# First factor of a Fourier transform: rows n1 and 47-n1 in separate 32x32 tiles, joined on VectorE

## The chip, the cores and the metric

The kernel runs on one core of one Trainium2 chip. The metric is device time in microseconds (us); all arithmetic is FP32. TensorE (PE in the profile) multiplies into PSUM banks, ScalarE (ACT) and VectorE (DVE) move and combine what stands there, GpSimd (POOL) and SyncE (SP) issue DMAs.

## The reference

Eight sequences of 3008 rows and 256 columns are filtered in the frequency domain, and the result goes through a two-layer network with an ELU in between.

```python
batch, seq, dim = (8, 3008, 256)          # x: batch x seq x dim
X = np.fft.rfft(x, axis=1)
F = (filt_r + 1j * filt_i)[None, :, :]    # seq // 2 + 1 frequencies
y = np.fft.irfft(X * F, n=x.shape[1], axis=1).astype(np.float32)
x = y.reshape(8 * 3008, 256)
h = x @ w_in                              # 256 -> 2048
g = np.where(h > 0.0, h, np.exp(np.minimum(h, 0.0)) - 1.0)
out = (g @ w_out).astype(np.float32)      # 2048 -> 256
```

## The kernel before

3008 is 47 x 64. The forward transform of a batch is made in two factors. The first (`a_unit`, line 236) multiplies the 64 rows n2 of one residue n1 by a table of 64 columns; rows n1 and 47-n1 use the same angles with opposite sign, so they are loaded together. The 24 pairs of residues are 6 chunks of 4 (`c` from 0 to 5). `x_load` (lines 205 to 216) brings a chunk into tile `xc` and its table into `ta`. `x_unit` (lines 222 and 223) forms on DVE the sum `sd` and the difference of the two halves of the 64 rows, which gives even and odd frequencies. Of a chunk's four pairs (slots), two lie on the lower and two on the upper 64 partitions; of each 64, 32 hold rows n1 and 32 rows 47-n1. `a_unit` takes two chunks and contracts those 64 together: the table has the columns cosine and sine twice, once with the sign that joins the two residues. The products land as 64x64 tiles, four at a time, in two banks per chunk, and ACT copies the four banks into two tiles `t1` (line 240). `z_write` (line 310) writes each chunk with two DMAs into the scratch `z` in DRAM, and `z_read` (line 316) reads it back transposed into the tile `t2`.

The second factor, `b_unit` (line 385), runs in sixteen 32x32 tiles at once, one bank for each row of tiles, ACT copies (line 390) and DVE sums (lines 403 and 404). `re_mult`, `re_sums`, `im_mult`, `im_join`, `im_sums` apply the filter on DVE, `bi_unit` (line 457) transforms back by the first inverse factor, again in sixteen tiles, `y_write` (line 468) and `y_read` (lines 487 and 491) pass through DRAM, and `n_unit` (line 524) makes the last inverse factor, six blocks `m` per batch, with sums on DVE (`n_sums`, lines 547 and 549).

The network works on blocks of 512 tokens by a seven-product scheme (Strassen's) in both layers. An item is one block `m` and one quarter `q` of the hidden layer, 24 items per batch. `up_steps` gives seven products into the banks called `s`, `a` and `d` (line 572), with copies on ACT (line 583), ELU exponentials on ACT (lines 589 and 590), sums (line 580) and maxima (line 594) on DVE and a tail of DVE differences (lines 630 to 634); `down_steps` gives seven products of the item before into four accumulators `po` (line 654), which are copied and joined (lines 659 and 670), transposed on DVE (line 693) and written out (line 703).

Four PSUM banks, handed out in a fixed order by the list `banks`, serve the up products and all transform stages; the other four are `po`.

The order is written out by hand. One loop step, called a quad in the code, interleaves the seven up products (U) of an item with the seven down products (D) of the item before. `at(quad, place, fn, ...)` plans other work into it: place 0 is the middle of the quad, place 1 its end, 2 and 3 points in between. A quad named in `opens` starts with D, because a stage at the end of the quad before has taken all four banks. The transform of batch `b` runs in the 24 quads in which the network works on batch `b - 1`; batch 0 has a transform of its own ahead of the loop (`a_first`, `b_first`, `bi_first`), beside which the weights are decoded (`w_split`, `w_float`, `w_join`, `w_sums`), some of that into the first quads of batch 1. Within a batch's 24 quads `a_unit` stands at the end of three quads, with `z_write`, `z_read` and the next `x_load`s behind it:

```python
for c, s in enumerate((2, 2, 3, 3, 4, 4) if b == 1 else (0, 0, 3, 3, 4, 4)):
    at(t + s, 0, x_unit, b, c)
    if c % 2 == 0:
        opens.add(t + s + 1)
        at(t + s, 1, a_unit, b, c)
```

`b_unit` stands at the end of quads 6, 10, 14 and 18, `bi_unit` at the end of quads 9, 13, 17 and 21, `n_unit` in the middle of quads 23, 1, 5, 8, 12 and 16. In all there are 21 `a_unit`s: three in each of batches 1 to 7.

## Time and profile before

| | |
|---|---|
| time, median of 3 runs | 2563.08 us (2561.91 to 2564.88) |
| the profiled execution: its span, first to last instruction | 2560.5 us |
| granted TensorE clock, mean of the span | 0.996 |
| PE, DVE, ACT busy | 98%, 81%, 60% of the span |
| L236 (`a_unit`), PE | 672 records of 0.38 us, up to four at once |
| L240, ACT copies of `a_unit` | 84 of 0.60 us |
| L222, L223, DVE, `x_unit` | 84 of 0.69 us |
| L403, L404, DVE sums of `b_unit` | 112 of 0.68 to 0.69 us |
| `z` written (SP) | 84 DMAs of 256 KB |
| `z` read into `t2` (SP) | 224 DMAs of 96 KB |

The profiled execution lies 2.6 us below the median of the runs, as its span leaves out what surrounds the instructions. The trace keeps records for each instruction, so an FP32 matmul appears as two records and two weight loads. The times in a timeline count from the first instruction of the span; the loop's first quad starts at about 87 us, quad 0 of batch 2 at about 397 us.

### The profile page before, as it was taken

What the parts mean: (1) busy time and instruction counts of PE and PEld (TensorE: products, weight loads), DVE (VectorE), ACT (ScalarE), POOL (GpSimd) and SP (SyncE); (2) the same over time, 40 slices, a digit from 0 to 9 for tenths busy, and PEclk for the clock granted to TensorE, in tenths of its full rate; (3) what the DMA queues carried; (4) which work ended last, traced back from release to release, by engine and by line L of the source; (5) the groups of instructions that cost most, each with busy time, mean ns of one, the idle gap of its engine ahead of it and who ended that gap; (6) DMA issues with size and microseconds to landing.
All of it is one profiled execution on the core that took longest, in us unless ns stands there. A gap on an engine that the chain in (4) does not pass through costs nothing.

```text
span 2560.5 us, 43982 instructions
## 1 busy us (share of the span) xinstructions
PE 2520.5 (98%) x16682; PEld 2161.5 (84%) x16682; DVE 2067.5 (81%) x3578; ACT 1545.2 (60%) x2715; POOL 159.5 (6%) x315
## 2 busy tenths in 40 slices
PE   6999999999999999999999999999999999999998
PEld 4788889888898888988889888888889888898887
DVE  6978887788878888788877888778897788876766
ACT  7766556655566555666566656566655665555554
POOL 5001000000000000000000000000100010000000
PEclk8999999999999999999999999999999999999999
DMA  9662223523233221433225231343213322110010
GB/s 283 182 184 67 58 45 79 131 62 71 48 100 97 69 66 40 128 80 72 52 52 142 66 77 36 77 123 80 66 39 84 88 62 63 37 45 18 20 27 17
DMA packets 229879, 200.56 MB, mean 78 GB/s; under 512 B 129398, under 2 KB 201990, under 8 KB 229668
## 3 DMA queue, kind: packets, MB, share of 16 engines
q1 hardware_dynamic: 214308, 166.86, 26.6%
q0 software_dynamic: 14000, 30.44, 4.2%
q8 instruction: 131, 2.15, 0.3%
q14 instruction: 80, 0.66, 0.1%
q10 hardware_dynamic: 1360, 0.46, 0.1%
HBM read 125.80 MB, written 78.12 MB: 80 GB/s over the span
## 4 chain that ended last, share of the span: by engine, by line
PE 97%; DMA 2%; DVE 1%; issue 0%; ACT 0%; SPq 0%; DVEq 0%; ACTq 0%
PE po L654 45%; PE phs L572 25%; PE phd L572 13%; PE pha L572 6%; PE psn L524 2%; PE psa L236 2%; PE pf L385 1%; PE pv L457 1%; DMA xc<-in_x_dram 1%; PE po L332 1%; DMA x<-in_x_dram 0%; PE po L298 0%; PE psr L332 0%; DMA t<-yd 0%; PE psa L279 0%
## 5 line engine op out<-in xcount | busy, mean ns | idle before, releaser
L654 PE MATMUL po<-g,wo 128*128 128x256 f32 (+1 forms) x5376 | 1317.6, 377 | 0.0
L654 PEld LDWEIGHTS po<-g,wo 128*128 128x128 f32 x5376 | 1010.7, 190 | 165.9 <-issue 49.8
L583 ACT ACTIVATE g<-phs 128x512 f32<-128x512 f32 (+1 forms) x576 | 338.7, 588 | 735.3 <-PE phs L572 733.3
L590 ACT ACTIVATE e<-e 128x512 f32<-128x512 f32 (+1 forms) x768 | 477.2, 621 | 24.3
L594 DVE SCALAR_TENSOR_TENSOR g<-e,g 128x512 f32<-128x512 f32 (+1 forms) x576 | 387.5, 673 | 13.6 <-ACT e L590 13.2
L580 DVE TENSOR_TENSOR g<-phd,g 128x512 f32<-128x512 f32 (+1 forms) x384 | 258.9, 674 | 166.2 <-ACT e L590 108.7
L572 PE MATMUL phs<-y,wi 128*128 128x256 f32 (+1 forms) x1536 | 387.6, 375 | 0.1
L572 PE MATMUL phd<-y,wi 128*128 128x256 f32 (+1 forms) x1504 | 380.3, 375 | 0.0
L589 ACT ACTIVATE e<-g 128x512 f32<-128x512 f32 (+1 forms) x576 | 354.4, 615 | 34.2 <-DVE g L580 26.7
L572 PEld LDWEIGHTS phs<-y,wi 128*128 128x128 f32 x1536 | 291.4, 190 | 33.6 <-ACT y L507 0.3
L572 PEld LDWEIGHTS phd<-y,wi 128*128 128x128 f32 x1504 | 284.8, 190 | 35.1 <-DVE g L580 2.7
L594 DVE SCALAR_TENSOR_TENSOR g<-e,phs 128x512 f32<-128x512 f32 (+1 forms) x192 | 129.8, 676 | 115.1 <-ACT e L590 115.1
L572 PE MATMUL phs<-yt,wi 128*128 128x256 f32 (+1 forms) x768 | 193.9, 375 | 0.9 <-ACT g L583 0.9
L572 PE MATMUL phs<-yb,wi 128*128 128x256 f32 (+1 forms) x768 | 193.9, 375 | 0.6 <-ACT g L583 0.6
L572 PE MATMUL pha<-yb,wi 128*128 128x256 f32 (+1 forms) x736 | 186.0, 375 | 0.0
L589 ACT ACTIVATE e<-phs 128x512 f32<-128x512 f32 (+1 forms) x192 | 112.2, 584 | 112.0 <-PE phs L572 112.0
L580 DVE TENSOR_TENSOR g<-pha,g 128x512 f32<-128x512 f32 (+1 forms) x192 | 129.5, 674 | 44.9 <-PE pha L572 44.9
L572 PEld LDWEIGHTS phs<-yt,wi 128*128 128x128 f32 x768 | 145.7, 190 | 18.0 <-ACT g L583 1.5
L572 PEld LDWEIGHTS phs<-yb,wi 128*128 128x128 f32 x768 | 143.1, 190 | 20.2 <-ACT g L583 1.0
L326 POOL DMA_DIRECT2D fall<-fp x224 | 110.1, 499 | 723.5 <-DVE r L430 697.7
L572 PEld LDWEIGHTS pha<-yb,wi 128*128 128x128 f32 x736 | 139.3, 190 | 16.7 <-ACT fall L394 0.5
L631 DVE TENSOR_TENSOR g<-g,g 128x512 f32<-128x512 f32 (+1 forms) x192 | 130.7, 681 | 6.7
(166 smaller groups left out, 2064.9 us busy)
## 6 DMA issues: line engine op xcount, KB each, us to landing
yd<-t SPq DMA_DIRECT2D x127, 192.0 KB
t<-yd SPq DMA_DIRECT2D x92, 256.0 KB
z<-t SPq DMA_DIRECT2D x84, 256.0 KB
fall<-fp POOLq DMA_DIRECT2D x224, 96.0 KB, 2.9
t<-z SPq DMA_DIRECT2D x224, 96.0 KB
out_dram<-o SPq DMA_DIRECT2D x632, 32.0 KB
xc<-in_x_dram SPq DMA_DIRECT2D x84, 128.0 KB
xc<-in_x_dram SPq DMA_DIRECT2D x161, 64.0 KB
```

The lines of the kernel that those rows point to most:

```text
L236: nc.tensor.matmul(p[o:o + 64, u, :], w[r, u, o:o + 64], src[r, u, :], start=True, stop=True)
L326: nc.gpsimd.dma_start(t[32 * a:32 * a + 24].rearrange("p c u d -> p (c u d)"), fp[g, a].rearrange("q c u d -> q (c u d)"))
L332: nc.tensor.matmul(ps[:, u:u + w, :], table[k, v, :], r[k, u:u + w, :], start=n == 0, stop=n == len(rhs) - 1)
L524: nc.tensor.matmul(p[ts(c, 64), dh, ts(q, 64)], t[r, i - 4 * m, ds(dh * P + 64 * c, 64)], w[r, i - 4 * m, :], start=True, stop=True)
L572: nc.tensor.matmul(ps[:, a, 0:h], w_in[q][:, COMBO[n], a, :], y[n], start=start and a == 0, stop=True, skip_group_check=True)
L580: nc.vector.tensor_tensor(out=g[o], in0=i0, in1=i1, op=ALU.add)
L583: nc.scalar.activation(out=g[o], in_=i0, func=AXT.Copy)
L589: nc.scalar.activation(out=e, in_=src, func=AXT.Relu, scale=-1.0)
L590: nc.scalar.activation(out=e, in_=e, func=AXT.Exp, scale=-1.0)
L594: nc.vector.scalar_tensor_tensor(out=g[n], in0=es[n], scalar=1.0, in1=src, op0=ALU.subtract, op1=ALU.max)
L631: nc.vector.tensor_tensor(out=b12, in0=b22, in1=b12, op=ALU.subtract)
L654: nc.tensor.matmul(po[i][:, u, 0:h], w_out[q][:, COMBO[n], a, :], g[n][:, a, :], start=q == 0 and a == 0 and n in (1, 3, 6, 4), stop=True, ...
```

## The change

Rows n1 and 47-n1 are no longer contracted in 64-row tiles with the joining sign in the table. Each of the four groups of 32 partitions (`k`: rows n1 and rows 47-n1 of the lower and of the upper two slots) is a row of 32x32 tiles with a bank of its own; the four columns of tiles are two chunks (`j`) by sum and difference (`o`). So the table `ta` keeps every second block of 32 columns (64 columns instead of 128). A unit issues 32 matmuls of 256 columns instead of 16, first those of rows 0 to 2, then those of row 3, for each of two slots `u`. Afterwards ACT copies two banks instead of four (1 and 3), and DVE forms the sum and the difference of each copied bank with its neighbour (0 and 2), into the tile `t1`, which now holds two slots of both chunks. The banks go back in the order 1, 3, 0, 2.

The scratch `z` becomes `[24, 2, 65, 256]`, sum and difference apart. `z_write` handles two chunks in one call, with eight DMAs of 128 KB instead of two times two of 256 KB; `z_read` takes the same four blocks of 24 rows from their new places. In batch 1 the three stages move by one quad, from quads 2, 3 and 4 to 3, 4 and 5; the other batches keep theirs.

```diff
-    ta = np.ascontiguousarray(tb).reshape(P, H // 2, P)
+    ta = np.ascontiguousarray(tb[..., 0::2, :]).reshape(P, H // 2, 64)
...
     def a_unit(b, c):
-        ps = [[bank("psa") for _ in range(2)] for _ in range(2)]
-        for j in range(2):
-            xt, w, sm = xs.pop((b, c + j)), tas.pop((b, c + j)), sds.pop((b, c + j))
-            for u in range(2):
-                for o, src in ((0, sm), (64, xt[:, 1])):
-                    for (_, p), r in zip(ps[j], HALVES):
-                        nc.tensor.matmul(p[o:o + 64, u, :], w[r, u, o:o + 64], src[r, u, :], start=True, stop=True)
-        for j in range(2):
-            t = t1s[b, c + j] = t1p.tile([P, XC, D], FP32, tag="t1", name="t1")
-            for h, (i, p) in enumerate(ps[j]):
-                nc.scalar.activation(out=t[:, 2 * h:2 * h + 2, :], in_=p, func=AXT.Copy)
-                banks.append(i)
+        ps = [bank("psa") for _ in range(4)]
+        src = [(tas.pop((b, c + j)), (sds.pop((b, c + j)), xs.pop((b, c + j))[:, 1])) for j in range(2)]
+        for u in range(2):
+            for rows in ((0, 1, 2), (3,)):
+                for j, (w, parts) in enumerate(src):
+                    for o in range(2):
+                        for k in rows:
+                            r, a = slice(32 * k, 32 * k + 32), 64 * j + 32 * o
+                            nc.tensor.matmul(ps[k][1][a:a + 32, u, :], w[r, u, 32 * o:32 * o + 32], parts[o][r, u, :],
+                                             start=True, stop=True, tile_position=(32 * k, a))
+        for h in range(2):
+            t = t1s[b, c, h] = t1p.tile([P, XC, D], FP32, tag="t1", name="t1").rearrange("p (u s) d -> p u s d", s=2)
+            one, two = ps[2 * h][1], ps[2 * h + 1][1]
+            nc.scalar.activation(out=t[:, :, 1], in_=two, func=AXT.Copy)
+            nc.vector.tensor_tensor(out=t[:, :, 0], in0=t[:, :, 1], in1=one, op=ALU.add)
+            nc.vector.tensor_tensor(out=t[:, :, 1], in0=one, in1=t[:, :, 1], op=ALU.subtract)
+        banks.extend(ps[k][0] for k in (1, 3, 0, 2))
...
     def z_write(b, c):
         if c == 0:
-            zs[b] = zp.tile([H, 4 * K2 + 1, D], FP32, tag="z", name="z")
-        t = t1s.pop((b, c))
-        z = zs[b][XC * c:XC * c + XC, 0:4 * K2, :].rearrange("i (q r) d -> r q i d", r=2)
-        for r in range(2):
-            nc.sync.dma_start(z[r], t[HALVES[r]])
+            zs[b] = zp.tile([H, 2, 2 * K2 + 1, D], FP32, tag="z", name="z")
+        for h in range(2):
+            t = t1s.pop((b, c, h)).rearrange("p u s d -> p (u s) d")
+            for j in range(2):
+                i = XC * (c + j) + 2 * h
+                z = zs[b][i:i + 2, :, 0:2 * K2, :].rearrange("i s (q r) d -> r q (i s) d", r=2)
+                for r in range(2):
+                    a = 64 * j + 32 * r
+                    nc.sync.dma_start(z[r], t[a:a + 32])
...
-                for c, s in enumerate((2, 2, 3, 3, 4, 4) if b == 1 else (0, 0, 3, 3, 4, 4)):
+                for c, s in enumerate((3, 3, 4, 4, 5, 5) if b == 1 else (0, 0, 3, 3, 4, 4)):
...
                     if c % 2:
-                        for k in (c - 1, c):
-                            at(t + s, 1, z_write, b, k)
+                        at(t + s, 1, z_write, b, c - 1)
```

More of the change, by code (lines that the diff above doesn't have):

```diff
@@ L201, in x_load @@
     def x_load(b, c, queue=nc.sync, place=None):
-        t, w = place or (xp.tile([P, 2, 2, D], FP32, tag="xc", name="xc"), tap.tile([P, 2, P], FP32, tag="ta", name="ta"))
+        t, w = place or (xp.tile([P, 2, 2, D], FP32, tag="xc", name="xc"), tap.tile([P, 2, 64], FP32, tag="ta", name="ta"))
         xs[b, c], tas[b, c] = t, w
@@ L305, in z_write @@
         if c == 0:
-            zs[b] = zp.tile([H, 4 * K2 + 1, D], FP32, tag="z", name="z")
-        t = t1s.pop((b, c))
-        z = zs[b][XC * c:XC * c + XC, 0:4 * K2, :].rearrange("i (q r) d -> r q i d", r=2)
-        for r in range(2):
-            nc.sync.dma_start(z[r], t[HALVES[r]])
+            zs[b] = zp.tile([H, 2, 2 * K2 + 1, D], FP32, tag="z", name="z")
[7 more added lines that the diff above has]
+                    nc.sync.dma_start(z[r], t[a:a + 32])
     def z_read(b, g):
         t = t2[:, g % 2]
-        for p in range(4):
-            k = p * K2 + 4 * g
+        for p, (n, k) in enumerate(((0, 0), (1, K2), (0, K2), (1, 0))):
             nc.sync.dma_start(t[32 * p:32 * p + 24].rearrange("i u d -> i (u d)"),
-                              zs[b][:, k:k + 4, :].rearrange("i u d -> i (u d)"))
+                              zs[b][:, n, k + 4 * g:k + 4 * g + 4, :].rearrange("i u d -> i (u d)"))
     def f_read_first(g, t):
```

## The prediction

> **What bounds the kernel now.** I read the page first: span, busy shares, chain.

> ```profile
> span 2560.5 us, 43982 instructions
> ...
> PE 2520.5 (98%) x16682; PEld 2161.5 (84%) x16682; DVE 2067.5 (81%) x3578; ACT 1545.2 (60%) x2715; POOL 159.5 (6%) x315
> ...
> PE 97%; DMA 2%; DVE 1%; issue 0%; ACT 0%; SPq 0%; DVEq 0%; ACTq 0%
> ```

> TensorE ends everything: 97% of the chain. What shortens PE's own stream counts in full; DVE, at 81%, has room on average but not in every quad (one step of the item loop: 12.1 us of L572 and L654 matmuls, plus what is planned into it). Next I read PE's timeline around one `a_unit` of batch 2:

> ```profile
> 457.21 0.43 PE L236 MATMUL psa<-sd,ta 64*64 64x256 f32 x2
> ...
> 458.79 0.38 PE L236 MATMUL psa<-xc,ta 64*64 64x256 f32 x2
> 459.10 1.13 PE L654 MATMUL po<-g,wo 128*128 128x256 f32 x4
> ```

> Every FP32 matmul is two records (passes), each with its own weight load. The stage takes 1.89 (457.21 to 459.10): eight waves of four records, 0.216 apart, the first 0.05 longer. Then the same view around two `bi_unit`s, which already run sixteen 32x32 tiles, and the weight loads inside the second one:

> ```profile
> 266.97 1.14 PE L457 MATMUL pv<-zs,pairs 24*32 24x512 f32 x32
> 268.04 1.13 PE L654 MATMUL po<-g,wo 128*128 128x256 f32 x4
> ```
> ```profile
> 214.49 1.29 PE L457 MATMUL pv<-zs,pairs 24*32 24x256 f32 x40
> 215.71 1.13 PE L654 MATMUL po<-g,wo 128*128 128x256 f32 x4
> ```
> ```profile
> 215.13 0.17 PEld L457 LDWEIGHTS pv<-zs,pairs 24*32 24x32 f32 x6
> ```

> Sixteen matmuls (32 records) of 512 columns take 1.07. The first `bi_unit` of a batch has twenty, with some of its columns in separate matmuls, and takes 1.22; six of its loads come as late as 215.13. Last, DVE after the third `a_unit` of batch 2, and PE, DVE and the SP queue in batch 1:

> ```profile
> 460.69 0.69 DVE L634 TENSOR_TENSOR g<-g,g 128x512 f32<-128x512 f32 x1
> ...
> 468.53 0.69 DVE L549 SCALAR_TENSOR_TENSOR yb<-y,y 128x512 f32<-128x512 f32 x1 [4.93 <-ACT y L531]
> ```
> ```profile
> 118.08 1.02 PE L572 MATMUL phd<-yb,wi 128*128 128x224 f32 x4 [1.67 <-DVE g L580]
> ```
> ```profile
> 158.85 0.69 DVE L549 SCALAR_TENSOR_TENSOR yb<-y,y 128x512 f32<-128x512 f32 x1 [4.93 <-ACT y L531]
> ```
> ```profile
> 152.61 3.72 SPq L310 DMA_DIRECT2D z<-t  x4
> 159.45 3.22 SPq L316 DMA_DIRECT2D t<-z  x8
> ...
> 171.28 12.11 SPq L703 DMA_DIRECT2D out_dram<-o  x24
> ```
> ```profile
> 175.07 1.72 PE L385 MATMUL pf<-t,pairs 24*32 24x256 f32 x40
> ```

> DVE idles 4.9 us in the quad after the third `a_unit`. Batch 1 is the exception: PE waits for DVE there (118.08), and from the `z_write`s (152.61) to the first `b_unit` (175.07) only 22 us pass.

> **The change, part by part.**

> *PE stage, 21 times.* 32 matmuls in 16 tiles: four waves of 256 columns instead of eight. Simply counted, the last pass starts 0.10 (16 tiles at 0.0067, as L457 issues them) + 0.267 + 2 x 0.216 = 0.80 after the start, and the next L654 follows 0.30 later, as today (458.79 to 459.10): 1.10, so 0.79 saved. But the 20-matmul `bi_unit` shows a limit. Its last three matmuls have idle tiles long before, yet their weight loads start only 0.64 us in (215.13, x6), 0.016 apart, 0.03 after the first matmul's second pass ends (it starts at 0.24, its record lasts 0.374). [...] That gives matmul 32 a first pass at 0.65 + 14 x 0.016 = 0.88, a second 0.24 later, and the next L654 at 1.42: **0.47 saved**. [...]

> *Bank waits.* The stage now needs its third bank at once and the fourth 12 matmuls later, not 0.9 us later. The fourth is freed by the L580 sum of `b21`. In the first two units of a batch that ends 0.6 to 0.8 before the stage; in the third it ends 0.31 after it, so row 3 starts at 0.36 and the stage takes 1.58: 0.31 saved. One steady batch: 2 x 0.47 + 0.31 = 1.24; six (b = 2 to 7) **7.4 us**.

> *Evacuation.* Per unit ACT loses two copies of 0.60, and DVE gains four operations like L403/L404 (0.68 and 0.69): 2.74 us, queued behind the tail (L634) and, in the third unit, the three L670 of `down_steps`. Behind them wait L580 (`b11`), the next `x_unit` and the `n_sums`. Steady, I price this at nothing, for what follows in the next quad waits anyway: DVE's idle time there, before the rows at 419.10, 448.53, 454.15 and 468.53, is 4.5 after unit 1, 1.85 + 2.27 after unit 2 and 4.9 after unit 3. Nor do the banks run out: `s1` wants the first one 2.4 after the stage's start (1.42 + 0.97 of L654) and ACT frees it at about 2.1; `n_unit` wants the one of the last sums 9.0 after it (147.53 to 156.52), and those end 7.7 after it. If that cover went, each of these quads would lose up to 2.7.

> *DMA and SP.* `ta` halves (42 x 64 KB less), hidden behind loads a quad ahead: nothing. `z_write` issues eight DMAs per pair instead of four, and waits for DVE's sums: in the third unit the L670s end at 462.2, so the halves are ready at 463.5 and 464.9 instead of 459.85. On SP behind it are `z_read`, `x_load`, the out DMAs and `y_read`. Steady, `t2` is then full at about 477 (463.5 + 1.3 + 12.4, today's time from first write to full), and `b_unit` is at 484.76: hidden, with 7 us to spare.

> *Batch 1, moved a quad later.* (a) Quad 2 loses `x_unit` and `a_unit`; the stall at 118.08 goes, but DVE is busy without a break to quad 3, where PE waits again, for the phd sum: 132.39 becomes about 130.75, since 0.9 of `x_unit`'s 2.74 is lost waiting for ACT's exp. (b) Unit 1 starts two matmul steps later, at 132.45, and unit 2 a quad later, at 145.45; PE then runs 2.4 ahead of today. (c) In quad 5 `x_unit` lies in DVE's queue behind `yb` (158.85 - 2.4 = 156.45, which waits for ACT): ended about 160.2, then L580 of `b22` at 160.85, for which PE's L572 waits 2.1. (d) Unit 3 runs from 162.6 to 164.05. From the sum of `b21` (162.7) the tail takes 3.8 and `n_sums` 1.2 as today, so its own sums end at 169.1 and 170.4. (e) First `z_write` to first `z_read`: 6.84 here, 6.66 in batch 2; eight reads take 3.2, the last issue lying 2.8 in, and land about 2.9 later (the row of `fall<-fp`, also 96 KB): 169.1 + 6.7 + 5.7 = **181.5** instead of being hidden. PE would be ready at 176.3 (164.05 + 12.1 + 0.1). So `b_unit` moves from 175.07 to 181.5: **6.4 lost**, its three cheaper units included. Ends: 4.9 late if the writes land as fast as the 290 GB/s seen at 152 to 154 us, 9 if they crawl. (f) The `y_read` for `n_unit` at 195.07 lies on SP behind `x_load` (6 to 8 us) and 24 out DMAs (12.1): issued about 198, landed 201 to 203, wanted at 201.5: 0 to 2, I take **0.5**.

> Sum: -7.4 + 6.4 + 0.5 = **-0.5**. The profiled span, 2560.5, becomes 2560.0; the three runs (2561.91 to 2564.88, median 2563.08) lie 2.6 above it, so 2562.6. A change within 0.2% (5.1 us) is what a measurement can hardly tell from none.

> **Rivals.**

> *The refill does not bind*: units take 1.10, 1.10 and 1.39. Batches 2 to 7 gain 12.4, batch 1 still loses 6.9, since its wait is for DMA: 2557.6. For it: tiles of `b_unit` and `bi_unit` overlap freely up to 16. Against: 215.13, and the 1.22 of every batch's first `bi_unit`. 0.13. [...]

> *The `z` round trip of batch 1 does not bind*, because the sums come earlier or the DMAs, now free of `f_read`'s traffic, land about 5 us sooner: -7.4 + 1.2 = -6.2, 2556.9. Against: 12.4 to 13.7 us from first write to full `t2` in both batches I looked at. 0.13.

> *Slower: SP's queue holds batch 1.* The third and fourth `z_write` of a group take 1.1 to 1.2 each on SP; if all eight do, the last starts at 177.5, reads follow 4.1 later, `t2` is full at 187.3 (12.2 late), and `y_read`, behind the same queue, makes `n_unit` wait 2: +14.3 - 7.4 = +6.9, 2570. It decides from a `b_unit` later than about 187. 0.15.

> *No gain in the stage*: the tiles do not run 16 at once and a unit stays at 1.89: +6.9, 2570. 0.04; `bi_unit`'s 1.07 speaks against it.

> **Numbers.** My forecast, a cancellation, has 0.55, with an own range of 2559 to 2567. Faster by over 0.2%: 0.13 + 0.13 = 0.26. Slower: 0.15 + 0.04 = 0.19. Same: 0.55. The range, 2556 to 2570, reaches the first three rivals; two gains at once (2552) stay outside.

> **What would show it.** `psa` stages of 1.42, 1.42 and 1.58 to the next L654 in batches 2 to 7, with loads of the second half from 0.65 on; DVE's L634-to-L549 gap down to about 2 without a PE wait; in batch 1 a wait of 2 at quad 5's phd and of about 5 at the first `b_unit`. Stages of 1.1, or no wait at that `b_unit`, prove me wrong on the fast side; PE waits after `a_unit` in steady batches, or a wait of 10 in batch 1, on the slow side.

## The result, and the profile after

The changed kernel takes 2566.38 us (median of 21 runs, 2561.00 to 2572.14) against 2562.87 (21 runs, 2561.14 to 2568.88) for the kernel before: a ratio of 1.0013, 95% interval 1.0007 to 1.0019, so 2 to 5 us slower. The forecast was 0.5 us faster, 2562.6, in a range of 2556 to 2570 that holds the time. The page of the profiled execution has the same balance as before; only PE's share of the chain that ended last falls from 97% to 95%:

```profile
span 2564.4 us, 45409 instructions
...
PE 2521.3 (98%) x17354; PEld 2159.8 (84%) x17354; DVE 2120.3 (83%) x3662; ACT 1525.5 (59%) x2673; POOL 159.6 (6%) x315
...
PE 95%; DMA 2%; DVE 1%; issue 0%; ACT 0%; SPq 0%; DVEq 0%; ACTq 0%
```

The lines of the code have moved: `a_unit`'s matmuls are L238, its DVE sums L244 and L245, the up products L580, their sums L588, the down products L662, `b_unit` L393, `z_write` L319, `z_read` L324. In a steady batch the trace shows what was forecast. PE's timeline of the third `a_unit` of batch 2 (start, duration, tile, records):

```profile
467.86 0.41 PE L238 MATMUL psa<-sd,ta 32*32 32x256 f32 x3
...
468.51 0.41 PE L238 MATMUL psa<-sd,ta 32*32 32x256 f32 x3
...
469.44 0.92 PE L662 MATMUL po<-g,wo 128*128 128x256 f32 x3
```

The seventeenth matmul starts 0.46 after the first, the other fifteen of the second half from 0.65 on (468.51), and the next L662 comes at 1.58. Over all 18 steady units the distances are 1.42 or 1.43 twice and 1.59 once a batch. DVE's timeline behind it, the last of the four new sums and the next quad's `yb`:

```profile
474.87 0.69 DVE L245 TENSOR_TENSOR t<-psa,t 128x512 f32<-128x512 f32 x1
...
478.88 0.69 DVE L557 SCALAR_TENSOR_TENSOR yb<-y,y 128x512 f32<-128x512 f32 x1 [2.00 <-ACT y L539]
```

The idle time ahead of `yb` has shrunk from 4.93 to 2.00, and no PE wait for another engine is listed from 215 us to 2540 us. So the sums on DVE are hidden.

The loss lies in batch 1. Compared quad by quad (the start of each quad's first up product in the two traces), the kernel after is 0.65 late before the first stage of batch 1, 11.57 late from quad 8 to the end of that batch, and 4.25 late at the last quad: +10.9 in batch 1, where 6.9 was forecast, and -7.3 in batches 2 to 7, where -7.4 was. PE's timeline in batch 1 (in brackets the wait and who ended it; `phd` is the tile in the bank called `d`, `phs` in `s`, `pf` that of `b_unit`):

```profile
131.25 1.02 PE L580 MATMUL phd<-yb,wi 128*128 128x224 f32 x4 [3.60 <-DVE g L588]
132.11 2.97 PE L662 MATMUL po<-g,wo 128*128 128x224 f32 x8
...
180.17 0.61 PE L393 MATMUL pf<-t,pairs 24*32 24x256 f32 x2 [0.62 <-DMA t<-z]
181.13 5.28 PE L393 MATMUL pf<-t,pairs 24*32 24x256 f32 x38 [0.34 <-DMA t<-z]
186.34 2.08 PE L662 MATMUL po<-g,wo 128*128 128x256 f32 x4
```

Eight L662 records took 2.97 after the first wait; the same eight took 1.68 in the kernel before (126.32). Four took 2.08 after the second, where 1.03 or 1.13 is usual. Nothing waits there; the clock is slower. The windows view shows it (stretch, length, PE busy and records, granted clock, DMA share, GB/s):

```profile
128.92:132.33 3.41, 1.08 (x6) 1.00 0.00 0
132.33:135.75 3.42, 3.42 (x40) 0.50 0.00 0
...
180.12:183.53 3.41, 2.97 (x12) 1.00 0.76 206
183.53:186.95 3.42, 3.42 (x32) 0.50 0.86 211
186.95:190.36 3.41, 3.41 (x10) 0.50 0.46 123
```

From 16 to 2555 us every stretch of one granted clock in this trace and in that of before lasts 3.41 us or a whole multiple of it; a piece of 3.41 us on this grid is called a window below. After each of the two long waits of batch 1 the granted clock is 0.50 (a half clock, below), for one window (132.33 to 135.75) and for two (183.53 to 190.36). The second wait shows only in part as one, 0.62 and 0.34: from 180.17 on `b_unit`'s tiles start singly, 12 records in 3.4 us, as their rows come. In the kernel before the clock stayed at 1.00 from 43 to 2555 us, and from 100 us on its longest PE wait was 1.67.

### The profile page after: what moved, and what is told of

Its sections match the earlier page's. It is cut to its first block, busy times and chain, and to the rows that moved or that the text cites. A ratio compares the mean times of both kernels' runs of the same rounds, so it can differ in the third digit from the quotient of the medians.

```text
span 2564.4 us, 45409 instructions
## 1 busy us (share of the span) xinstructions
PE 2521.3 (98%) x17354; PEld 2159.8 (84%) x17354; DVE 2120.3 (83%) x3662; ACT 1525.5 (59%) x2673; POOL 159.6 (6%) x315
## 4 chain that ended last, share of the span: by engine, by line
PE 95%; DMA 2%; DVE 1%; issue 0%; ACT 0%; SPq 0%; DVEq 0%; ACTq 0%
PE po L662 44%; PE phs L580 25%; PE phd L580 12%; PE pha L580 6%; PE psn L532 2%; PE pf L393 2%; PE pv L465 1%; PE psa L238 1%; DMA xc<-in_x_dram 1%; DMA x<-in_x_dram 0%; DMA yd<-t 0%; PE po L340 0%; PE po L303 0%; DMA z<-t 0%; PE psr L340 0%
## 5 line engine op out<-in xcount | busy, mean ns | idle before, releaser
L662 PE MATMUL po<-g,wo 128*128 128x256 f32 (+1 forms) x5376 | 1319.9, 377 | 0.0
L662 PEld LDWEIGHTS po<-g,wo 128*128 128x128 f32 x5376 | 1012.0, 190 | 167.5 <-issue 53.4
L602 DVE SCALAR_TENSOR_TENSOR g<-e,g 128x512 f32<-128x512 f32 (+1 forms) x576 | 387.6, 673 | 13.7 <-ACT e L598 13.3
L588 DVE TENSOR_TENSOR g<-phd,g 128x512 f32<-128x512 f32 (+1 forms) x384 | 259.1, 675 | 160.2 <-ACT e L598 110.2
L580 PE MATMUL phs<-y,wi 128*128 128x256 f32 (+1 forms) x1536 | 388.4, 375 | 0.0
L580 PE MATMUL phd<-y,wi 128*128 128x256 f32 (+1 forms) x1504 | 380.3, 375 | 0.0
L580 PEld LDWEIGHTS phs<-y,wi 128*128 128x128 f32 x1536 | 292.0, 190 | 33.5 <-ACT g L591 0.2
L580 PEld LDWEIGHTS phd<-y,wi 128*128 128x128 f32 x1504 | 284.8, 190 | 35.1 <-DVE g L588 2.7
L580 PE MATMUL phs<-yt,wi 128*128 128x256 f32 (+1 forms) x768 | 193.8, 375 | 0.9 <-ACT g L591 0.9
L580 PE MATMUL phs<-yb,wi 128*128 128x256 f32 (+1 forms) x768 | 193.9, 375 | 0.6 <-ACT g L591 0.6
L580 PE MATMUL pha<-yb,wi 128*128 128x256 f32 (+1 forms) x736 | 186.0, 375 | 0.0
L580 PEld LDWEIGHTS phs<-yt,wi 128*128 128x128 f32 x768 | 145.7, 190 | 17.9 <-ACT g L591 1.3
L580 PEld LDWEIGHTS phs<-yb,wi 128*128 128x128 f32 x768 | 143.1, 190 | 20.2 <-ACT g L591 1.0
L580 PEld LDWEIGHTS pha<-yb,wi 128*128 128x128 f32 x736 | 139.3, 190 | 16.7
L588 DVE TENSOR_TENSOR g<-pha,g 128x512 f32<-128x512 f32 (+1 forms) x192 | 129.4, 674 | 28.3 <-PE pha L580 28.3
```

The source lines that it names most:

```text
L580: nc.tensor.matmul(ps[:, a, 0:h], w_in[q][:, COMBO[n], a, :], y[n], start=start and a == 0, stop=True, skip_group_check=True)
L588: nc.vector.tensor_tensor(out=g[o], in0=i0, in1=i1, op=ALU.add)
L602: nc.vector.scalar_tensor_tensor(out=g[n], in0=es[n], scalar=1.0, in1=src, op0=ALU.subtract, op1=ALU.max)
L662: nc.tensor.matmul(po[i][:, u, 0:h], w_out[q][:, COMBO[n], a, :], g[n][:, a, :], start=q == 0 and a == 0 and n in (1, 3, 6, 4), stop=True, ...
```

## The experiments

My theory after seeing this: the mechanisms of the forecast hold, but in this kernel a PE wait of some 3.5 us costs the wait and about half of each 3.41 us window at 0.50 behind it. Rivals: the new unit itself is at fault; or only the move by a quad is.

**e1, the move alone.** The kernel before, with its own units, in quads 3, 4 and 5.

```diff
-                for c, s in enumerate((2, 2, 3, 3, 4, 4) if b == 1 else (0, 0, 3, 3, 4, 4)):
+                for c, s in enumerate((3, 3, 4, 4, 5, 5) if b == 1 else (0, 0, 3, 3, 4, 4)):
```

> The old 64x64 unit, with batch 1's three units moved by one quad and nothing else. Theory A (moving batch 1 is what costs; the new unit itself gains 7.3 us in batches 2 to 7): 5 to 9 us slower than before, with a PE wait of 2 to 4 us in quad 3, one of about 2 in quad 5, and the first b_unit of batch 1 waiting for t2 little or not at all, since no DVE sums stand ahead of z_write. Theory B (the loss comes from the DVE sums and the eight writes, the move costs nothing): within 2 us of before.

Measured: 2570.07 (2568.77 to 2572.55), ratio 1.0030 (1.0018 to 1.0041). The same wait of 3.60 at quad 3's phd, followed by a clock of 0.50 at 132.53 to 135.95, and one of 2.0 at quad 5; no wait at `b_unit`. Instead PE waits for `y_read`'s rows at `n_unit`, for 1.10 and 0.76, which I had put at 0.5:

```profile
202.75 0.30 PE L524 MATMUL psn<-tn,t 64*64 64x64 f32 x2 [1.10 <-DMA t<-yd]
```

A second half clock follows (204.21 to 207.63). Batch 1 costs 9.6 here, 3.8 of it from quad 8 to quad 9. So the move alone makes batch 1 dear; what the new unit costs it without the move, e2 shows.

**e2, the new unit alone.** The kernel after, with batch 1's stages back in quads 2, 3 and 4 (the same edit the other way round).

> The changed kernel with batch 1's units back in quads 2, 3 and 4. Theory A: the gain of 7.3 us stays, and the DVE sums make PE wait another 3 to 6 us in quads 3 and 4 of batch 1, perhaps with a fall of the clock: 1 to 4 us faster than before. Theory B: no better than the changed kernel, 3 us slower than before or more.

Measured: 2559.46 (2557.17 to 2562.18), ratio 0.9990 (0.9981 to 0.9999). PE waits 1.67 at quad 2's phd, as before, and 3.71 at quad 3's: ahead of the sum that PE waits for (136.23) DVE has the decoding of weights, the four new sums (129.15 to 131.87) and two `x_unit`s (133.58 to 136.31). A half clock follows that wait (137.64 to 141.05). Batch 1 costs 3.4, batches 2 to 7 gain 7.4.

**e3, the clock kept up.** The kernel after, with idle full-array matmuls in the two waits, none of which PE needed for anything else.

```diff
+    def keep_warm(n):
+        ps = psM.tile([P, 512], FP32, tag="m%d" % banks[0], name="warm")
+        for _ in range(n):
+            nc.tensor.matmul(ps, w_in[0][:, 0, 0, :], w_in[0][:, 0:2].rearrange("p a b c -> p (a b c)"),
+                             start=True, stop=True)
...
         def s4():
+            if (b, m, q) == (0, 0, 3):
+                keep_warm(4)
...
+                    if b == 1 and g == 0:
+                        at(s, 1, keep_warm, 5)
                     at(s, 1, b_unit, b, g)
```

> The changed kernel with nine idle 128x512 matmuls that PE does in two of its waits of batch 1: four ahead of the phd product in quad 3, five ahead of the first b_unit. Theory A with the clock (the granted clock was 0.50 for 3.4 us after the first wait and for 6.8 us after the second; about 5 us of the loss is this): the clock stays at 1.0 after 90 us and the kernel gains 3 to 5 us on the changed one, ending within 2 us of before. Rival (the half clock only fell into waits and cost nothing): same as the changed kernel, or slower by up to 1.

Measured: 2563.53 (2561.39 to 2566.24), ratio 1.0005 (0.9996 to 1.0014). No half clock after either wait. But PE, now earlier at quad 8, meets the wait for `y_read` there, and that one brings a half clock of its own (203.13 to 206.54):

```profile
201.56 0.29 PE L538 MATMUL psn<-tn,t 64*64 64x64 f32 x2 [0.93 <-DMA t<-yd]
202.62 1.60 PE L538 MATMUL psn<-tn,t 64*64 64x64 f32 x62 [0.76 <-DMA t<-yd]
```

From quad 8 to quad 9 the kernel falls back by 3.7. So by the ratios it gains 2 us on the kernel after and not the 3 to 5 expected, and the two intervals overlap. Two waits of under 1 us were enough for a half clock this time, while 2.02 at quad 5's phd was not in any kernel so far: the length of a wait alone did not decide here.

**e6, that third wait taken away too.** e3, with the table and the rows for this `n_unit` issued on SP a quad earlier, ahead of the 24 output DMAs.

```diff
-                    at(t + s - 2, 0, tn_read, b, m)
-                    at(t + s - 2, 1 if m == 0 else 0, y_read, b, m)
+                    e = t + s - 3 if (b, m) == (0, 3) else t + s - 2
+                    at(e, 0, tn_read, b, m)
+                    at(e, 1 if m == 0 else 0, y_read, b, m)
```

> The kernel of e3_keep_warm, with the loads for the fourth n_unit of batch 0 (its table and y_read) issued on SP a quad earlier, ahead of the 24 output DMAs of the first o_unit. Theory A (the third wait was y_read standing behind those DMAs, and the half clock after it is a window of 3.41 us in which PE was busy for under half): no wait at that n_unit, no half clock between 88 and the end; e3 lost 3.66 from quad 8 to quad 9, so 2563.5 - 3.7 = 2559.9, ratio about 0.999 to before. Rival B (the DMA traffic as such, not the place in SP's queue, makes the rows late): the wait stays near 1 + 0.8 and so does the time, 2563.5.

Measured: 2560.97 (2559.81 to 2564.19), ratio 0.9998 (0.9989 to 1.0007). `n_unit` waits no more, the clock is 1.00 from 87 to 2555 us, and nothing is lost between quads 8 and 9. The windows around `b_unit`:

```profile
179.21:182.62 3.41, 3.35 (x46) 1.00 0.73 198
182.62:186.04 3.42, 3.42 (x17) 1.00 0.49 140
```

Batch 1 costs 6.75 and batches 2 to 7 gain 7.3. With the half clocks gone the kernel stands where the forecast put it, level with the kernel before.

**e10, the same idle matmuls in one small tile.** e6's kernel again, the idle matmuls as many and as long, but in one 32x32 tile.

```diff
-            nc.tensor.matmul(ps, w_in[0][:, 0, 0, :], w_in[0][:, 0:2].rearrange("p a b c -> p (a b c)"),
-                             start=True, stop=True)
+            nc.tensor.matmul(ps[0:32], w_in[0][0:32, 0, 0, 0:32], w_in[0][0:32, 0:2].rearrange("p a b c -> p (a b c)"),
+                             start=True, stop=True, tile_position=(0, 0))
```

> The kernel of e6_warm_read with the idle matmuls (four in quad 3, five ahead of the first b_unit) made in one 32x32 tile instead of the whole array: as many, as long (two passes of 0.43 us), as busy in the profile, a sixteenth of the array's work. Theory A (what sets the clock is work by array area: counting each record with 0.84 ns per column times rows x columns of its tile over 128 x 128, every window of 3.41 us so far with up to 1.29 us of it was followed by 0.50, every one with 1.31 or more was not): the waits count as idle again, so a half clock follows the wait in quad 3 and the one at b_unit, unless a window's edge halves such a wait; the time goes from e6's 2561.0 towards after's 2566.4: 2563.5 to 2567. Rival B (what counts is whether PE is busy, whatever the tile): no half clock between 90 and 2540, 2561 as e6.

Measured: 2566.45 (2563.99 to 2576.57), ratio 1.0016 (1.0005 to 1.0026), the loss of the kernel after. Batch 1 costs 11.3 in its trace, against 6.75 in e6's. The windows view (first row quad 3, the others around `b_unit`) shows PE busy throughout, and ahead of `b_unit` the half clock follows all the same:

```profile
129.32:132.74 3.42, 3.36 (x14) 1.00 0.00 0
...
180.52:183.94 3.42, 3.36 (x21) 1.00 0.89 206
183.94:187.35 3.41, 3.41 (x42) 0.50 0.83 197
```

In quad 3 no half clock followed: the window's edge at 129.32 cut that stretch in two, and each side had 1.5 to 1.6 us of full-array work by the count further down, under e7; the expectation had named that exception. Instead the 2.02 of quad 5's phd, hurting nobody so far, fell into one window (1.28 us of work) and was followed by a half clock.

**e7, waits made on purpose.** The kernel before, with DVE delayed ahead of one b21 sum in every eleventh quad.

```diff
         def s4():
+            i = 24 * b + 4 * m + q
+            if i >= 56 and i % 11 == 1:
+                for _ in range(4 + i // 11 % 6):
+                    nc.vector.tensor_tensor(out=g["b21"], in0=g["t2"], in1=g["t2"], op=ALU.add)
```

> Before's kernel with 4 to 9 extra DVE additions (0.69 us each, into the tile of b21 that the next one overwrites) ahead of the b21 sum in 12 to 13 quads, 11 apart, from quad 56 on, so that PE waits at phd for lengths from about 1 to 6 us at 12 phases. Theory A (the clock is set for each window of 3.41 us on one fixed grid: a window in which PE is busy for less than about half, 1.7 us, is followed by one at 0.50): waits under 1.7 are never followed by a half clock, waits over 3.4 always, those between by where they lie on the grid; every window with under 1.70 busy is followed by 0.50 and none with over 1.80. Rival B (only a wait longer than a whole window, or a window without any matmul, halves the clock): waits of 2 to 3.4 never do.

Measured: 2639.91 us, one run. In the trace (the waits fall at other products than phd too) PE's waits over 3.41 us (eight, 3.73 to 5.41) were all followed by a half clock, 2.36 and 2.67 were too, 2.28, 1.21 and 1.12 were not. That refutes B: two waits shorter than a window were followed by a half clock. A's bound on busy time fails as well. Five windows at half clock with 1.91 to 3.00 busy were followed by another half, and among the windows at full speed it has one miss, the first of these rows (busy 1.50, and the clock stays); the third window, quite as busy, is followed by 0.50:

```profile
1565.04:1568.45 3.41, 1.50 (x7) 1.00 0.00 0
1568.45:1571.86 3.41, 0.13 (x1) 1.00 0.00 0
...
1114.48:1117.89 3.41, 1.57 (x11) 1.00 0.19 34
1117.89:1121.30 3.41, 2.89 (x35) 0.50 0.22 41
```

The two differ in what PE did. In the first it was full-array matmuls, in the third partly `b_unit`'s 24x32 tiles. So I counted work by area, an estimate from the records: 0.84 ns per column of each record (256 columns in 0.216), times rows x columns of its tile over 128 x 128. In the profiles of before, after, e1 to e4 and e6 to e9, from 50 to 2540 us, the 22 full-speed windows with the least work (0 to 1.29 us) are all followed by 0.50, and every other one (1.31 us and more) by 1.00. e10, run after this count, added two on the one side (0.23 and 1.28) and none on the wrong one. How sharp the border between the two groups is depends on the count: with each record's work put 0.1 us earlier or later, two windows lie on the wrong side, and the border is anywhere from 1.2 to 1.4. The weight by area is clearer. Weighted by the rows of a tile alone, 54 windows followed by 1.00 have less work than the fullest one followed by 0.50, and by its columns alone 259; by area none has. The row of after at 180.12, followed by 0.50, fits the count too: 2.97 busy, but with single tiles of `b_unit` waiting for rows, and 0.12 us of work.

**e8, one wait less.** e6 with the third `x_unit` of batch 1 ahead of `n_sums` in DVE's stream.

```diff
                     at(t + s, 0, x_unit, b, c)
+                    if b == 1 and s == 5:
+                        plan[5, 0].insert(c - 4, plan[5, 0].pop())
```

> e6_warm_read with one step moved: in quad 5 the x_unit of the third unit of batch 1 stands ahead of the n_sums in DVE's stream, so that it fills the idle time before yb. Theory A (the wait at quad 5's phd is the 2.7 us of x_unit behind yb, and everything after it hangs on that sum): the wait of about 2 at phd goes or falls below 0.7, the third unit's sums end about 1.3 to 2.7 earlier, t2 is full as much earlier, and the first b_unit comes 1.3 to 2.7 sooner: 2557.2 to 2558.6 if e6 is at 2559.9, that is 0.05 to 0.1% under e6. Rival B (the first b_unit is held by something else than those sums, SP or the DMA rings): the phd wait goes, but the wait at b_unit grows by as much and the time is e6's.

Measured: 2561.72 (2558.56 to 2564.59), ratio 0.9994 (0.9986 to 1.0003), which can't be told from e6; 1.3 to 2.7 less was expected. In the trace the wait at quad 5's phd is gone (0.2 left). Net of the start, which is 0.78 later here than in e6's trace, the third unit's sums end 2.1 earlier, but the first `b_unit` gives part of it back:

```profile
178.69 2.58 PE L399 MATMUL pf<-t,pairs 24*32 24x256 f32 x40
```

It starts 2.1 earlier, net, than in e6 (180.05), in both traces where the idle matmuls end, and lasts 2.58 instead of 1.77, as its rows trickle in: the way from the first `z_write` to the first `z_read` took 6.73 in e8 and 6.17 in e6. So `b_unit` hangs partly on the sums (theory A) and partly on the DMAs behind them (B). Measured from quad 1 to quad 24 the gain is 1.1, which the spread of the runs hides.

**e5 and e9, the order of the tiles.** The kernel after, with the two slots of one tile issued one behind the other.

```diff
-        for u in range(2):
-            for rows in ((0, 1, 2), (3,)):
-                for j, (w, parts) in enumerate(src):
-                    for o in range(2):
-                        for k in rows:
+        for rows in ((0, 1, 2), (3,)):
+            for j, (w, parts) in enumerate(src):
+                for o in range(2):
+                    for k in rows:
+                        for u in range(2):
```

> After's kernel with the order of the 32 matmuls of a unit turned: the two slots u of one 32x32 tile follow each other, instead of sixteen tiles with u = 0 and then sixteen with u = 1. [...] 18 steady units x 0.5 to 0.75 = +9 to +13.5, batch 1 another +1 to +2: 2576 to 2582. Rival B (tiles are independent and the order of issue does not matter): 1.42 stays and the time is after's, 2566.

> The kernel of e5_slots_inner once more, for a profile of an ordinary run (the one of e5_slots_inner was taken in a run of 10727 us). Theory A: a unit of batches 2 to 7 takes 1.9 to 2.2 to the next matmul (2578.5 to 2588 us in the runs of e5 agrees), its first 16 matmuls go two deep into 8 tiles, tiles 9 to 12 start at about 0.5 and tiles 13 to 16 at about 0.95. Rival B: the units take 1.42 and the time is lost elsewhere.

Measured: e5 2578.47 to 2587.99 in three runs, ratio 1.0078 (1.0062 to 1.0095); a fourth execution, the profiled one, took 10727 us, which I have not explained and leave out. e9 took 2582.70. PE's timeline of the third unit of batch 2 in e9:

```profile
471.98 0.42 PE L238 MATMUL psa<-sd,ta 32*32 32x256 f32 x3
...
473.06 0.46 PE L238 MATMUL psa<-xc,ta 32*32 32x256 f32 x3
...
474.23 1.13 PE L662 MATMUL po<-g,wo 128*128 128x256 f32 x4
```

Every steady unit takes 2.25, more than the old unit's 1.89. The seventeenth matmul, in the ninth tile, still starts early, at 0.43. Number 19, the first of the tenth tile, starts at 1.08 (473.06). Number 2 is now the second slot of the first tile: its passes start at 0.46 and 0.67, and the record of the second ends at 1.05, 0.03 before number 19 starts. In the units of after (the one at 467.86, say) number 18 starts at 0.65, 0.03 after the record of number 1's second pass ends (0.62). In both places the later matmul starts 0.03 after the record of the one 17 places ahead has ended. So theory A had the order right but not the times: the tiles 10 to 16 start from 1.08 to 1.28, not in groups at 0.5 and 0.95, and the unit takes a little more than the 2.2 expected. The same 32 matmuls, in 16 tiles at once, cost 1.42 or 2.25 by their order. Rival B, independent tiles, is out.

**e4, a version that beats both.** The new unit in batches 2 to 7; batch 1 with the old unit, table, `z` and quads.

```diff
+    def a_unit_one(b, c):
+        ...
     def a_unit(b, c):
+        if b == 1:
+            return a_unit_one(b, c)
...
-                for c, s in enumerate((3, 3, 4, 4, 5, 5) if b == 1 else (0, 0, 3, 3, 4, 4)):
+                for c, s in enumerate((2, 2, 3, 3, 4, 4) if b == 1 else (0, 0, 3, 3, 4, 4)):
```

> The new unit in batches 2 to 7; batch 1 keeps the old unit, its table of 128 columns, its layout of z and its quads 2, 3 and 4. Theory A: all of the gain and none of the loss: 7 to 7.5 us faster than before (ratio 0.997), with no fall of the clock after the loop has begun. Theory B (the sums and writes cost something that a batch's trace hides): 0 to 4 us faster.

Measured: 2552.97 (2552.53 to 2556.02), ratio 0.9966 (0.9954 to 0.9979). The waits view of PE from 100 us on has one row, the two waits of the kernel before, and the clock is 1.00 from 38 to 2547 us:

```profile
PE phd L610 <- DVE g L618: 2.3, 2, 1.7
```

Quad by quad, batch 1 costs 0.0 and batches 2 to 7 gain 7.4, as forecast for them. Another 2.2 of the profiled run lie ahead of the loop, in the start, which lies between 2.3 earlier and 1.9 later than that of the kernel before in the traces kept.

## Why the prediction was wrong

**The stage on PE** (1.42, 1.42, 1.58): right, to 0.01. The refill, the late start of the second half's weight loads, was read from one group of loads (215.13) and accounts for the difference between 1.10 and 1.42: with it number 32 was put at 0.65 + 14 x 0.016 = 0.88, and in the units of after number 18 starts at 0.65 and number 19 at 0.67. In that `bi_unit`, too, the seventeenth matmul's first pass starts 0.46 in, ahead of the late group. e9 shows a late start by another route. What holds the loads back no run shows; the runs show when they start, 0.03 after the matmul 17 places ahead has ended, in the `bi_unit`, in after and in e9. Without a refill batches 2 to 7 would have gained 12.4, as the rival has it; they gained 7.3.

**Evacuation and DMAs in steady batches at nothing, and the bank wait**: right. The gap ahead of `yb` fell to 2.00, and b21's sum delayed only the third unit, as priced.

**Batch 1, (a) to (e)**: the waits were right, their price was not. Net of the 0.65 at the start, quad 3's phd came at 130.60 (forecast 130.75), the wait at quad 5 was 2.02 (2.1), and (e) from the first `z_write` to the first `z_read` passed 5.70 (6.7; eight writes took 3.75 on SP, as four took 3.72 before). Two things failed:

- The step that failed is the price of (a) and (e). I let PE run at full speed after a wait of 3.6 and after one of some 5 us. The half clocks cost 1.6 behind quad 3's phd (the L662 records late by 1.3, unit 1 lasting 1.78 instead of 1.42) and about 2.9 from 183.53 on, 4.5 together. Of the 2.9, 1.97 is seen directly: from 186.34 the next three groups of four records took 4.66 to 191.00, where 0.97 + 0.86 + 0.86 is usual; 0.88 is an estimate for `b_unit`, whose last 25 records took 1.94 up to the next L662 (from 184.40), where the same 25 in e8 took 1.06 (from 180.15). The pair e10 and e6, differing only in the tile of the idle matmuls, gives as much: batch 1 costs 4.6 more in e10's trace, with half clocks at quad 5 and behind `b_unit`, and the ratios, 1.0016 and 0.9998, are as far apart.
- In (b) I left out one L662 step. A quad that doesn't open with D has two D steps between that phd and its `a_unit`. So unit 1 came at 134.35 and not 132.45, net of the start: 0.76 for that step, the rest the half clock.

Sum: 6.9 + 4.5 + 0.8 - 1.0 (writes) - 0.5 (f) = 10.7, against 10.9 measured. Without the half clocks it would be 6.2. That e6, at 6.75, comes so near the forecast's 6.9 is therefore in part luck, as three errors partly cancel; and since `b_unit` starts there where the idle matmuls end (179.98), some of the 6.75 may be theirs, which is not shown.

**(f), `y_read`**: nothing in the kernel after, where `b_unit` came so late that the rows were there. e1 and e3 show it was mis-sized: with PE earlier there, it cost 1.7 to 1.9 of waiting and a half clock, 3.7 to 3.8 in all.

**Rivals.** "The refill does not bind" and "no gain in the stage" are refuted by units of 1.42. "SP's queue holds batch 1" had the right sign and place, not the mechanism: the eight writes of the third unit took no longer than the four before. "The round trip doesn't bind" is refuted, by the wait at `b_unit` and by the rows that trickle in in e8.

The length of a wait, on which my theory after the result rested, did not decide the clock in these runs: two gaps of 0.93 and 0.76 us beside matmuls in 64x64 tiles were followed by 0.50 (e3), one of 2.28 us between full-array matmuls was not (e7).

## What to carry to other kernels

Price a PE wait with the clock behind it. In the kernel after, the wait of 3.60 at quad 3's phd cost another 1.6 us (one window at 0.50) and the waits at `b_unit` 2.9 us (two), both partly estimates. Waits of 2.36 and 2.67 (e7), and 0.93 and 0.76 beside 64x64 tiles (e3), were followed by a half clock too. Where the windows lay made a difference: the wait of 2.02 at quad 5's phd was followed by one in e10, where it fell into one window, and by none in the kernel after, where the edge at 163.05 cut it. That may be why the runs of the kernel after spread from 2561 to 2572; no run shows it. A change that pays in the steady part need not be applied where its resources are scarce; leaving batch 1 alone turned a loss of 3.5 us into a gain of 9.4, 7.4 of it in the loop. When many small tiles are issued, try independent tiles first and a second use of a tile late: this unit of 32 FP32 matmuls took 1.42 us so, and 2.25 with the two uses of a tile one behind the other (e9).
